# An attention, a dense layer and eight weighted experts on one core: the block products of the experts' second projection in another order

## The chip, the cores and the metric

The kernel runs on one core of a Trainium2 chip. The metric is the device time of one execution in microseconds. A core has five engines with instruction streams of their own: TensorE (PE; PEld is its weight load), VectorE (DVE), ScalarE (ACT), GpSimd (POOL) and SyncE (SP). Each works through its list in order and waits on semaphores for the others. Transfers are issued by SyncE's queue and by GpSimd's.

## The reference

Three stages follow one another, in fp32:

```
scores = q k^T / 8 + bias(i, j)          # 2 x 8 heads, 576 positions, 64 wide
attn   = softmax(scores);  x = attn v    # x: 1152 tokens x 512
g = softplus(x w_in);  x = g w_out       # 512 -> 2048 -> 512
P = exp(x w_gate - max)                  # 1152 x 8 shares
8 times: rows of P to sum 1, columns to sum 1, P *= 1152 / 8
out = sum over e of P[:, e] * (relu(x w1[e]) w2[e])   # 512 -> 1024 -> 512
```

The bias is a two-layer network of log-distances, the same for both batches.

## The kernel before, in words

**Stages.** A first stage makes the bias tables and writes them to DRAM (`wt`), from where they are read as `bias` tiles; the list `READS` says after which of 40 steps which part of a tile is read on SyncE's queue. Attention follows. The two feed-forward stages are cut into 40 units of 256 hidden columns: units 0 to 7 are the dense layer, 8 to 39 the experts, four units each. Unit 8 to 11 (expert 0) also computes the shares `P`: its small steps stand in a table `gate`, and `ask(u, "a2")` and its like run the step of a place in a unit (r0 to r2 in the first projection, a0 to a3 and b0 to b3 in the second). The last step is `publish` (L1204): the shares go to DRAM and are read back spread over all partitions, `raw<-pt` for expert 0 and `pb<-pt` for the next expert.

**Precision.** Every fp32 operand is held as a high and a low part (`hi` and `lo`, or the indices 0 and 1). ScalarE copies the high part (`first`), and VectorE or GpSimd subtracts it from the whole to get the low one (`second`). A product is three matmuls: high·high, high·low, low·high (`TRIPS`). For weights from unit 12 on the low part is made differently (`parts`, L726): ScalarE writes the high part and its negative, and a GpSimd DMA adds the source to the negative in SBUF.

**First projection.** 1024 tokens times 256 columns are done as seven products of half the size (Strassen's scheme in Winograd's form), numbered 1 to 7 in `PRODUCTS`, in the order `UP` = 1, 2, 6, 5, 7, 3, 4, 0. Each is six matmuls of 512 columns. They run up in three PSUM banks X, Y, Z; ScalarE copies intermediate sums out (`keep`), VectorE adds (`add`). Number 0 is `up_last`: the remaining 128 tokens, twelve matmuls of 256 columns, tile `gl`.

**Second projection of the fast units (12 to 38).** The four blocks of the result, B22, B11, B12 and B21, come out of `weighted` already clipped and multiplied by the tokens' shares `pb`. The second projection is again seven block products (`DOWN`): A11·B11, S1·T1, S2·T2, S4·B22, S3·T3, A12·B21, A22·T4, with T1 = B12 − B11, T2 = B22 − T1, T3 = B22 − B12, T4 = B21 − T2 of the tokens and S1 to S4 of the weights (`mixd`, four GpSimd instructions). Banks X and Z (tile `sum`) take them in turns X, Z, X, Z, X, Z, X, and VectorE adds a bank into `acc` after every product (L982, 128x1024), so that a later product on a bank waits for that addition. Product 1 of the next unit runs ahead of the first block product. `turn_last` transposes the last tokens, `down_last` multiplies them (tile `pv`) and adds.

**Order.** The schedule is manual: on each engine instructions stand as the code issues them. Weights come by SyncE (`f<-in_e_w`), are mixed on GpSimd (`mix`, `mixd`) and split (`high`, `highd`, `highs`); `FAST_JOBS` and `DOWN_JOBS` say after which product each of these is issued. At the start of unit 12 the sums of expert 0 are multiplied by its shares (`weigh_columns`, one instruction of 128x2048 on GpSimd and one on VectorE).

**Last unit.** `down_out` adds the projected tokens to the transposed `acc`: per 128 tokens six matmuls and four 128x128 products with the identity (L1018), then a copy and a DMA out.

Of the kernel before, what the change touches and what calls it, by code (L numbers as in the profile page):

```python
# [56 lines left out]
READS = ((30, 2, ((0, 576),)), (31, 1, ((0, 512),)), (32, 0, ((0, 384),)), (33, 4, ((192, 576),)), (34, 3, ((128, 576),)),  # L57
         (36, 1, ((512, 576),)), (38, 0, ((384, 576),)), (39, 4, ((0, 192),)), (39, 3, ((0, 128),)))
# [42 lines left out]
WDAT = {"A12": (0, 0), "A22": (0, 256), "A11": (0, 512), "S3": (1, 768), "S1": (1, 0), "S2": (1, 256), "S4": (1, 512)}  # L101
WAT = {"B11": 0, "B21": 512, "B22": 640, "T1": 1024, "T4": 1152, "T3": 1536, "T2": 1664}
# [10 lines left out]
def attention_moe_moe_kernel(ctx: ExitStack, tc, qT, kT, vN, wpos, w_in, w_out, w_gate, e_w1, e_w2,  # L113
# [503 lines left out]
    def experts(m0, accp, xr):  # L617
# [246 lines left out]
        def weighted(u, n, src):  # L864
# [16 lines left out]
            elif n == 7:  # L881
                first(name)
            elif n == 3:
# [86 lines left out]
        def down_fast(u):  # L970
# [3 lines left out]
            for at, (n, x, a, b, (c, i)) in enumerate(DOWN):  # L974
                m, o = WDAT[a]
                ws = wss if m else [wd(u)[:, 0], wd(u)[:, 1]]
                for k, (wo, ho) in enumerate(((0, 0), (1, 0), (0, 1))):
                    for f in range(2):
                        nc.tensor.matmul(banks[x][:, f], ws[wo][:, o + 128 * f:o + 128 * f + 128], h[b][:, ho],  # L979
                                         start=(n in (1, 5, 2) and k == 0), stop=(k == 2), skip_group_check=True)  # L980
                d = acc[c][:, 2 * i:2 * i + 2]
                nc.vector.tensor_tensor(out=d, in0=banks[x], in1=d, op=ALU.add)  # L982
                if at == 0:
                    difference(nc.vector, "T4", "B21", "T2")
                    first("T4")
                    second(nc.gpsimd, "T4")
                if at == 2:
                    turn_last(u)
                if at == 4:
                    down_last(u)  # L990
                if at == 3:
                    after(u + 1, 1)
                for what, ahead, k in DOWN_JOBS.get(at, ()):
                    if u + ahead < NU:
                        weights[what](u + ahead, k)
# [4 lines left out]
        def weigh_columns(c):  # L1000
            d = acc[c]
# [316 lines left out]
        def unit(u):  # L1318
# [64 lines left out]
            else:  # L1383
                for n, p in enumerate(UP):
# [7 lines left out]
                    if n > 4:  # L1392
                        ask(u, f"r{n - 5}")
# [226 lines left out]
```

## Time and profile before

| | |
|---|---|
| median of 3 runs | 1222.6 us (1222.27 to 1222.66) |
| profiled execution | 1223.38 us, span of its instructions 1221.6 us |
| busy in the span | PE 95%, DVE 77%, ACT 60%, POOL 68% |
| units 0 to 39 | from about 250 us on; the fast units from 542 to 1188 us |
| mean granted clock of TensorE | 0.994 of 2.4 GHz |

All times below are microseconds from the start of the span. A row of the timeline gives the start, the duration, the engine, the line and the tiles (output<-inputs); in brackets stands how long the engine had been idle before it, and what ended that. In a list of waits a row says which instruction waited for which, the sum, the number and the longest.

### The profile page before, as it was taken

To read this page: it belongs to the slowest core of one execution; us is meant where nothing else is said; L and a number is where in the kernel's file an instruction comes from. 1 tells how busy PE (TensorE), PEld (TensorE's weight loads), DVE (VectorE), ACT (ScalarE), POOL (GpSimd) and SP (SyncE) were. 2 spreads that over 40 slices of the span, in tenths; PEclk is the share of its full clock that TensorE was granted. 3 is DMA by queue.
4 is the path that set the end of the run, shared out by engine and by line. 5 is a ranking of instruction groups with operands and counts; after the bars stand their busy time and mean duration, and the time that the engine had idled before them with its cause. 6 is when DMAs were issued, how large, how long until landed. Compare 5 with 4: busy or idle time off the path is not lost.

```text
span 1221.6 us, 19900 instructions
## 1 busy us (share of the span) xinstructions
PE 1165.7 (95%) x7321; PEld 967.4 (79%) x7321; DVE 943.1 (77%) x1470; ACT 735.6 (60%) x1190; POOL 825.8 (68%) x827
## 2 busy tenths in 40 slices
PE   5989999999999999997999999999999999999998
PEld 5878999888888868776777777777777777777777
DVE  9977888588887674647887788778778878778873
ACT  7966887775445544255566656656666565565642
POOL 8226777667887935337777777768777777877850
PEclk9999999999999999998999999999999999999999
DMA  5768663032223201064765765766576577467552
GB/s 138 226 187 233 210 195 107 1 102 89 88 86 104 87 18 52 1 124 97 155 139 125 155 136 126 154 144 132 125 156 151 113 154 164 104 141 173 118 104 78
DMA packets 82873, 152.42 MB, mean 125 GB/s; under 512 B 9360, under 2 KB 47448, under 8 KB 82776
## 3 DMA queue, kind: packets, MB, share of 16 engines
q0 software_dynamic: 15984, 58.20, 26.4%
q1 hardware_dynamic: 66360, 92.51, 24.8%
q8 instruction: 58, 0.95, 0.3%
q10 hardware_dynamic: 432, 0.45, 0.1%
q14 instruction: 39, 0.32, 0.1%
HBM read 78.79 MB, written 14.14 MB: 76 GB/s over the span
## 4 chain that ended last, share of the span: by engine, by line
PE 57%; POOL 14%; DVE 12%; DMA 8%; issue 7%; ACT 2%; SPq 0%; POOLq 0%; DVEq 0%; ACTq 0%
PE sum L1038 10%; PE sum L979 9%; PE t L814 9%; DMA wu<-f 6%; PE op L543 5%; PE pv L814 4%; POOL h L857 3%; PE sps L452 3%; PE pv L1054 3%; POOL f L750 3%; PE pac L268 3%; PE tail L814 3%; PE tp L502 3%; DVE f L860 2%; POOL raw L857 2%
## 5 line engine op out<-in xcount | busy, mean ns | idle before, releaser
L982 DVE TENSOR_TENSOR acc<-sum,acc 128x1024 f32<-128x1024 f32 x189 | 228.7, 1220 | 40.7 <-PE sum L979 34.0
L814 PE MATMUL t<-room,wu 128*128 128x512 f32 x592 | 172.1, 396 | 7.1 <-DMA wu<-f 5.9
L1038 PE MATMUL sum<-h,wd 128*128 128x512 f32 x576 | 138.6, 394 | 0.0
L814 PEld LDWEIGHTS t<-room,wu 128*128 128x128 f32 x592 | 107.6, 188 | 37.9 <-DMA wu<-f 17.0
L853 ACT ACTIVATE raw<-f 128x512 fp32r<-128x512 f32 x81 | 51.2, 633 | 131.7 <-DVE f L860 131.7
L1038 PEld LDWEIGHTS sum<-h,wd 128*128 128x128 f32 x576 | 105.5, 188 | 21.7 <-DVE acc L1071 0.5
L814 PE MATMUL pv<-x,wu 128*128 128x512 f32 x444 | 114.5, 394 | 7.3 <-ACT u L842 7.3
L728 ACT ACTIVATE wu<-f 128x1024 fp32r<-128x1024 f32 x77 | 81.2, 1054 | 39.3 <-POOL f L724 32.6
L814 PEld LDWEIGHTS pv<-x,wu 128*128 128x128 f32 x444 | 83.8, 190 | 25.7 <-ACT u L842 8.1
L731 POOL DMA_DIRECT2D wu<-f x56 | 57.5, 1028 | 64.6 <-ACT h L853 43.7
L857 POOL TENSOR_TENSOR raw<-f,raw 128x512 fp32r<-128x512 f32 x54 | 70.2, 1300 | 34.9 <-ACT raw L853 34.9
L837 DVE TENSOR_TENSOR u<-t,u 128x512 f32<-128x512 f32 x37 | 25.6, 691 | 85.5 <-PE t L814 84.3
L814 PE MATMUL t<-x,wu 128*128 128x512 f32 x296 | 85.2, 389 | 0.0
L733 POOL TENSOR_TENSOR wu<-f,wu 128x1024 fp32r<-128x1024 f32 x21 | 53.0, 2524 | 45.2 <-ACT wu L728 44.6
L268 PE MATMUL pac<-bw,m 128*128 128x64 bf16 (+1 forms) x1920 | 66.6, 198 | 17.4 <-DVE bw L240 12.4
L979 PE MATMUL sum<-h,wd 128*128 128x512 f32 x324 | 82.5, 390 | 0.0
L857 POOL TENSOR_TENSOR h<-u,h 128x512 fp32r<-128x512 f32 x54 | 81.0, 1519 | 0.0
L268 PEld LDWEIGHTS <-m 128*128 128x128 bf16 (+1 forms) x1920 | 63.1, 105 | 20.8 <-issue 8.6
L1071 DVE TENSOR_TENSOR acc<-sum,acc 128x512 f32<-128x512 f32 x80 | 55.0, 688 | 25.8 <-PE sum L1038 25.4
L979 PE MATMUL sum<-h,raw 128*128 128x512 f32 x216 | 65.5, 405 | 9.3 <-DVE acc L982 9.0
L728 ACT ACTIVATE raw<-f 128x1024 fp32r<-128x1024 f32 x27 | 28.6, 1061 | 74.9 <-POOL f L750 74.9
L979 PEld LDWEIGHTS sum<-h,wd 128*128 128x128 f32 x324 | 60.8, 188 | 13.2
(297 smaller groups left out, 3172.8 us busy)
## 6 DMA issues: line engine op xcount, KB each, us to landing
f<-in_e_w_dram SPq DMA_DIRECT2D x128, 256.0 KB, 4.2
wu<-f POOLq DMA_DIRECT2D x56, 512.0 KB, 5.4
wd<-f POOLq DMA_DIRECT2D x28, 512.0 KB, 4.6
room<-f POOLq DMA_DIRECT2D x27, 512.0 KB, 5.0
raw<-in_w_in_dram SPq DMA_DIRECT2D x16, 512.0 KB, 3.6
raw<-in_w_out_dram SPq DMA_DIRECT2D x16, 512.0 KB, 3.6
bias<-wt SPq DMA_DIRECT2D x13, 576.0 KB, 5.5
raw<-in_qT_dram SPq DMA_DIRECT2D x16, 288.0 KB, 5.9
```

The lines of the kernel that those rows point to most:

```text
L268: nc.tensor.matmul(pt[0:n, g], lhs, win(w, (k * (ng + 1) + gw) * NC, [[(ng - gw) * NC, 2], [1, NC]]), start=(k == 0), stop=(k == 2))
L543: nc.tensor.matmul(op[:, 0:n], l, r, start=(part == 0 and k == 0), stop=(part == 8))
L728: nc.scalar.activation(hi, src, AF.Copy)
L731: nc.gpsimd.dma_start(out=lo.bitcast(F32), in_=src, accum_op=ALU.add)
L733: nc.gpsimd.tensor_tensor(out=lo, in0=src, in1=hi.bitcast(F32), op=ALU.subtract)
L814: nc.tensor.matmul(zz, wu(u)[:, a, o:o + 128], xs[xn][b][j], start=(n in (1, 2, 5) and k == 0), stop=(k == 5), skip_group_check=True)
L853: nc.scalar.activation(h[name][:, 0], full[name], AF.Copy)
L857: eng.tensor_tensor(out=t[:, 1], in0=full[name], in1=t[:, 0].bitcast(F32), op=ALU.subtract)
L979: nc.tensor.matmul(banks[x][:, f], ws[wo][:, o + 128 * f:o + 128 * f + 128], h[b][:, ho], start=(n in (1, 5, 2) and k == 0), stop=(k == 2) ...
L982: nc.vector.tensor_tensor(out=d, in0=banks[x], in1=d, op=ALU.add)
L1038: nc.tensor.matmul(s, lhs, rhs, start=(n == 0), stop=(n == 5))
L1071: nc.vector.tensor_tensor(out=d, in0=o, in1=d, op=ALU.add)
```

## The change

It edits the fast units, the steps for the shares and the last unit, and one table of the bias stage.

- `READS`: parts of the same bias tile are read together and later; seven reads in place of nine.
- Fast units run `up_last` before product 4 (`UP_FAST`).
- B22's low part is issued with product 7; T3 is issued after T2's low part; T4 moves from VectorE to GpSimd; T3's and B21's parts are issued after the first block product.
- The first block product runs one half of the bank after the other, and VectorE adds each half by itself (128x512). `turn_last` moves from the third to the first block product. The last tokens' sum moves from after the fifth to after the third, its addition to the end.
- The weight jobs get other places: `high(u+1, 1)` from the first projection to after the first block product, `mixd` from the fifth to the second, `high(u+2, 0)` from the seventh to the fourth, `highs` and `mix` to the sixth.
- `weigh_columns` becomes four pieces of 128x1024, all on VectorE, from the third step of unit 12 on.
- The steps of the shares stand two or three places sooner, so that `publish` is at a2 of unit 11 instead of b1.
- The identity products of the last unit become transposes in TensorE's transposing form and come first.
- The last low part of the dense layer's output is made on GpSimd.

```diff
-READS = ((30, 2, ((0, 576),)), (31, 1, ((0, 512),)), (32, 0, ((0, 384),)), (33, 4, ((192, 576),)), (34, 3, ((128, 576),)),
-         (36, 1, ((512, 576),)), (38, 0, ((384, 576),)), (39, 4, ((0, 192),)), (39, 3, ((0, 128),)))
+READS = ((30, 2, ((0, 576),)), (31, 1, ((0, 512),)), (34, 0, ((0, 384),)), (36, 1, ((512, 576),)), (39, 0, ((384, 576),)),
+         (39, 3, ((0, 576),)), (39, 4, ((0, 576),)))
...
+UP_FAST = (1, 2, 6, 5, 7, 3, 0, 4)
...
             elif n == 7:
                 first(name)
+                second(nc.gpsimd, "B22")
             elif n == 3:
...
                 difference(nc.vector, "T2", "B22", "T1")
-                difference(nc.gpsimd, "T3", "B22", "B12")
                 first("T1")
                 first("T2")
-                first("T3")
                 second(nc.vector, "T1")
                 second(nc.gpsimd, "T2")
-                second(nc.gpsimd, "B22")
-                second(nc.gpsimd, "T3")
+                difference(nc.gpsimd, "T3", "B22", "B12")
             else:
                 h["T4"] = tss[2]
                 first(name)
-                second(nc.gpsimd, "B21")
...
+                order = [(k, f) for k in range(3) for f in range(2)] if at else [(k, f) for f in range(2) for k in range(3)]
...
+                for fs_ in (slice(0, 2),) if at else (slice(0, 1), slice(1, 2)):
+                    d = acc[c][:, 2 * i:2 * i + 2][:, fs_]
+                    nc.vector.tensor_tensor(out=d, in0=banks[x][:, fs_], in1=d, op=ALU.add)
                 if at == 0:
-                    difference(nc.vector, "T4", "B21", "T2")
+                    turn_last(u)
+                    difference(nc.gpsimd, "T4", "B21", "T2")
+                    first("T3")
+                    second(nc.gpsimd, "T3")
+                    if u > U1 + UE:
+                        weights["high"](u + 1, 1)
                     first("T4")
+                    second(nc.gpsimd, "B21")
                     second(nc.gpsimd, "T4")
-                if at == 2:
-                    turn_last(u)
-                if at == 4:
-                    down_last(u)
                 if at == 3:
                     after(u + 1, 1)
+                if at == 2:
+                    r = last_sum(u, "pv")
+                if at == 6:
+                    evac(u, 2, 0, r)
...
-        slots = slots[slots.index((1, "b0")):]
+        slots = slots[slots.index((1, "a1")):]
...
+                for j in range(4):
+                    nc.tensor.matmul(s[:, 128 * j:128 * j + 128], acc[c][:, j, cols], ident, start=(j == 0), stop=False,
+                                     is_transpose=True, skip_group_check=True)
...
-                        if n == 1:
-                            for j in range(4):
-                                nc.tensor.matmul(s[:, 128 * j:128 * j + 128], acc[c][:, j, cols], ident, start=False, stop=False)
...
-        FAST_JOBS = {3: (("high", 1),)}
-        DOWN_JOBS = {4: (("mixd", 1, 0), ("highd", 1, 0), ("highs", 1, 0), ("mix", 2, 0)), 6: (("high", 2, 0),)}
+        DOWN_JOBS = {1: (("mixd", 1, 0),), 3: (("high", 2, 0),), 4: (("highd", 1, 0),), 5: (("highs", 1, 0), ("mix", 2, 0))}
...
-                    if u == U1 + UE and n == 1:
-                        for c in range(2):
-                            weigh_columns(c)
+                    if u == U1 + UE and 1 < n < 6:
+                        weigh_columns(n % 2, n // 4)
```

GpSimd's list in one fast unit, before. `u<-v,u` is T3, `raw<-f,raw` the low part of T2 and at the end of T4, `h<-v,h` that of B22, `h<-u,h` those of T3 and B21; the two L750 rows are `mixd`; the DMA rows add a low part of weights (wd and room of the next unit); L721 begins `mix`:

```order
L860 TENSOR_TENSOR u_8604<-v_8538,u_8604 128x512
L857 TENSOR_TENSOR raw<-f_4649,raw 128x512
L857 TENSOR_TENSOR h<-v_8538,h 128x512
L857 TENSOR_TENSOR h<-u_8604,h 128x512
L857 TENSOR_TENSOR h<-u_8614,h 128x512
L857 TENSOR_TENSOR raw<-f_4649,raw 128x512
L750 TENSOR_TENSOR f_4651<-f_4650 128x256 x2
L750 TENSOR_TENSOR f_4651<-f_4651,f_4650 128x256
L750 TENSOR_TENSOR f_4651<-f_4650,f_4651 128x256
L731 DMA wd_4648<-f_4650 128x1024
L731 DMA room<-f_4651 128x1024
L721 TENSOR_TENSOR f_2605<-f_2604 128x2x2x128
```

The same list in the changed kernel, from B22's low part on:

```order
L858 TENSOR_TENSOR h<-v_8556,h 128x512
L858 TENSOR_TENSOR raw<-f_4646,raw 128x512
L861 TENSOR_TENSOR u_8611<-v_8556,u_8611 128x512
L861 TENSOR_TENSOR f_4646<-u_8621,f_4646 128x512
L858 TENSOR_TENSOR h<-u_8611,h 128x512
L732 DMA wu_4644<-f_2602 128x1024
L858 TENSOR_TENSOR h<-u_8621,h 128x512
L858 TENSOR_TENSOR raw<-f_4646,raw 128x512
L751 TENSOR_TENSOR f_4648<-f_4647 128x256 x2
L751 TENSOR_TENSOR f_4648<-f_4648,f_4647 128x256
L751 TENSOR_TENSOR f_4648<-f_4647,f_4648 128x256
L732 DMA wu_2599<-f_2601 128x1024
```

T4 (`f<-u,f`) is new in it, T3 has moved behind T2's low part, one weight transfer (`wu<-f`) now stands ahead of `mixd` and another directly behind it.

VectorE's list in a fast unit, before, from T2 (`f<-v,f`) on: T1's low part, B21 out of PSUM, the additions into `acc`, T4 between the first two of them, and `hl`, the low part of the last tokens:

```order
L860 TENSOR_TENSOR f_4649<-v_7610,f_4649 128x512
L857 TENSOR_TENSOR raw<-f_4649,raw 128x512
L874 SCALAR_TENSOR_TENSOR u_7686<-t,pb 128x512
L982 TENSOR_TENSOR acc<-sum,acc 128x1024
L860 TENSOR_TENSOR f_4649<-u_7686,f_4649 128x512
L982 TENSOR_TENSOR acc<-sum,acc 128x1024 x2
L913 SCALAR_TENSOR_TENSOR hl<-tail,hl 128x256
L982 TENSOR_TENSOR acc<-sum,acc 128x1024 x2
L1073 SCALAR_TENSOR_TENSOR acc<-pv,prob,acc 128x512
L982 TENSOR_TENSOR acc<-sum,acc 128x1024 x2
```

And in the changed kernel:

```order
L861 TENSOR_TENSOR f_4646<-v_7623,f_4646 128x512
L858 TENSOR_TENSOR raw<-f_4646,raw 128x512
L875 SCALAR_TENSOR_TENSOR u_7688<-t,pb 128x512
L982 TENSOR_TENSOR acc<-sum,acc 128x512 x2
L911 SCALAR_TENSOR_TENSOR hl<-tail,hl 128x256
L982 TENSOR_TENSOR acc<-sum,acc 128x1024 x6
L1083 SCALAR_TENSOR_TENSOR acc<-pv,prob,acc 128x512
```

T4 is gone from between the additions, the first addition is two halves, and the last tokens' addition has moved to the end.

VectorE's list at the start of the first fast unit (12), before; `acc<-acc,raw` is the weighing, `tail<-tail,v` the addition behind product 2, `v<-tail,pb` B22:

```order
L1071 TENSOR_TENSOR acc<-pv,acc 128x512
L1002 TENSOR_TENSOR acc<-acc,raw 128x2048
L837 TENSOR_TENSOR tail<-tail,v_7100 128x512
L874 SCALAR_TENSOR_TENSOR v_7100<-tail,pb 128x512
L837 TENSOR_TENSOR u_7133<-t,u_7133 128x512
```

And in the changed kernel:

```order
L1081 TENSOR_TENSOR acc<-pv,acc 128x512
L838 TENSOR_TENSOR tail<-tail,v_7097 128x512
L875 SCALAR_TENSOR_TENSOR v_7097<-tail,pb 128x512
L1008 TENSOR_TENSOR acc<-acc,raw 128x1024 x3
L838 TENSOR_TENSOR u_7130<-t,u_7130 128x512
L875 SCALAR_TENSOR_TENSOR u_7130<-u_7130,pb 128x512
L1008 TENSOR_TENSOR acc<-acc,raw 128x1024
```

Product 2's addition and B22 now stand before the weighing, three quarters of which stand before product 7's addition.

## Rows read from the trace of the kernel before

**Rows 1.** What TensorE waited for, whole span: us in total, times, longest.
```profile
PE sum L979 <- DVE acc L982: 9.0, 20, 0.7
PE pv L814 <- ACT u L842: 7.3, 1, 7.3
PE t L814 <- DMA wu<-f: 5.9, 13, 1.7
```

**Rows 2.** The line of the differences: ns min/median/max, first and last start; T1, T3, T2.
```profile
L860 DVE TENSOR_TENSOR f<-u,u x27: 691/691/693, 560.8 to 1172.6; 128x512 f32<-128x512 f32 x27
L860 POOL TENSOR_TENSOR u<-v,u x27: 1646/1657/1672, 561.6 to 1173.4; 128x512 f32<-128x512 f32 x27
L860 DVE TENSOR_TENSOR f<-v,f x27: 1761/1771/1787, 562.0 to 1173.8; 128x512 f32<-128x512 f32 x27
```

**Rows 3.** Timeline of the second projection of one fast unit: start, us, engine.
```profile
845.68 0.76 PEld L814 LDWEIGHTS t<-room,wu 128*128 128x128 f32 x4 [0.56 <-DMA wu<-f]
...
846.49 1.34 PEld L979 LDWEIGHTS sum<-h,wd 128*128 128x128 f32 x6
...
846.76 0.68 DVE L857 TENSOR_TENSOR raw<-f,raw 128x512 fp32r<-128x512 f32 x1
...
848.30 1.22 DVE L982 TENSOR_TENSOR acc<-sum,acc 128x1024 f32<-128x1024 f32 x1 [0.26 <-PE sum L979]
...
848.84 1.29 POOL L857 TENSOR_TENSOR h<-v,h 128x512 fp32r<-128x512 f32 x1
...
849.44 1.23 DVE L860 TENSOR_TENSOR f<-u,f 128x512 f32<-128x512 f32 x1
849.64 0.30 PEld L979 LDWEIGHTS sum<-raw 128*128 128x128 f32 x2 [0.44 <-issue]
...
850.59 2.34 DVE L982 TENSOR_TENSOR acc<-sum,acc 128x1024 f32<-128x1024 f32 x2
...
850.90 0.37 PEld L965 LDWEIGHTS tail<-ident,gl 128*128 128x128 f32 x2
...
851.86 0.30 PEld L979 LDWEIGHTS sum<-h,raw 128*128 128x128 f32 x2 [0.59 <-DVE acc L982]
...
854.49 1.32 PEld L1054 LDWEIGHTS pv<-wd,hl 128*128 128x128 f32 x6
...
855.85 1.32 PEld L979 LDWEIGHTS sum<-h,wd 128*128 128x128 f32 x6
```

**Rows 4.** Two stretches: us, busy of PE, PEld, DVE, ACT, POOL, PEclk, DMA share.
```profile
617.00:1162.00 545.00, 530.03 (x2409) 425.80 (x2409) 436.30 (x487) 328.71 (x462) 417.96 (x420) 1.00 0.65 139
...
556.00:566.00 10.00, 9.69 (x42) 8.06 (x42) 8.97 (x10) 5.47 (x9) 6.17 (x5) 0.83 0.41 99
```

**Rows 5.** Timeline of GpSimd's transfers in the same unit, and their ScalarE conversion.
```profile
857.27 1.06 ACT L728 ACTIVATE raw<-f 128x1024 fp32r<-128x1024 f32 x1 [2.90 <-POOL f L750]
...
859.81 0.86 POOL L731 DMA_DIRECT2D room<-f  x1 [1.76 <-issue]
860.37 1.62 POOL L721 TENSOR_TENSOR f<-f 128x512 f32<-128x512 f32 x1
...
863.70 1.20 POOL L731 DMA_DIRECT2D wu<-f  x1
```

**Rows 6.** The chain that ended last, first fast unit: start, us, what.
```profile
542.63 10.58 DMA pb<-pt
...
556.31 2.94 PE pv L814 x6
```

**Rows 7.** Timeline of VectorE there.
```profile
551.49 2.29 DVE L1002 TENSOR_TENSOR acc<-acc,raw 128x2048 f32<-128x2048 f32 x1 [8.50 <-DMA raw<-pt]
```

**Rows 8.** Timeline of TensorE's weight loads in the last unit.
```profile
1197.58 1.09 PEld L1018 LDWEIGHTS sum<-ident,acc 128*128 128x128 f32 x8
1198.59 1.23 PEld L1014 LDWEIGHTS sum<-wd,h 128*128 128x128 f32 x6
```

**Rows 9.** Timeline of VectorE at the start of attention.
```profile
90.04 0.76 DVE L465 CUSTOM_DVE_ANT_0 p<-sps,bias 128x576 f32<-128x576 f32 x1 [1.61 <-PE tp L502]
```

More of the change, by code (lines that the diff above doesn't have):

```diff
@@ L976, in down_fast @@
                 ws = wss if m else [wd(u)[:, 0], wd(u)[:, 1]]
[L977 to L982, printed above, removed]
[L983 to L984 removed]
+                order = [(k, f) for k in range(3) for f in range(2)] if at else [(k, f) for f in range(2) for k in range(3)]
+                for k, f in order:
+                    wo, ho = ((0, 0), (1, 0), (0, 1))[k]
+                    nc.tensor.matmul(banks[x][:, f], ws[wo][:, o + 128 * f:o + 128 * f + 128], h[b][:, ho],
+                                     start=(n in (1, 5, 2) and k == 0), stop=(k == 2), skip_group_check=True)
+                for fs_ in (slice(0, 2),) if at else (slice(0, 1), slice(1, 2)):
+                    d = acc[c][:, 2 * i:2 * i + 2][:, fs_]
+                    nc.vector.tensor_tensor(out=d, in0=banks[x][:, fs_], in1=d, op=ALU.add)
+                if at == 0:
+                    turn_last(u)
[4 more added lines that the diff above has]
+                        weights["high"](u + 1, 1)
                     first("T4")
+                    second(nc.gpsimd, "B21")
                     second(nc.gpsimd, "T4")
[L987 to L990 removed]
                 if at == 3:
                     after(u + 1, 1)
+                if at == 2:
+                    r = last_sum(u, "pv")
+                if at == 6:
+                    evac(u, 2, 0, r)
                 for what, ahead, k in DOWN_JOBS.get(at, ()):
@@ L1046, in down, with last_sum @@
                     x_next(c, k)
-        def down_last(u):
+        def last_sum(u, name):
             w = wd(u).rearrange("p o (t f) -> p o t f", t=2)
             weigh(u, 2)
-            r, n, t = bank("pv") if u != U1 - 1 else ps2("sumr")[:, 0], 0, h["last"]
+            r, n, t = bank(name) if name == "pv" else ps2(name)[:, 0], 0, h["last"]
             for f in range(2):
@@ L1320, in jobs @@
                 if U1 <= u + 1 < NU:
-                    for what, k in (FAST_JOBS if fast(u) else JOBS if u >= U1 else FIRST).get(n, ()):
+                    for what, k in ({} if fast(u) else JOBS if u >= U1 else FIRST).get(n, ()):
                         weights[what](u + 1, k)
@@ L1383, in unit @@
             else:
-                for n, p in enumerate(UP):
-                    if u == U1 + UE and n == 1:
-                        for c in range(2):
-                            weigh_columns(c)
+                for n, p in enumerate(UP_FAST if fast(u) else UP):
+                    if u == U1 + UE and 1 < n < 6:
+                        weigh_columns(n % 2, n // 4)
+                    if u == U1 + UE and n == 5:
                         tss.extend(again(k, [128, 2, 512], F32R) for k in range(3))
@@ L1391, in unit @@
                             weights[what](u + 1, 0)
+                    if n == 3 and u == U1 + UE:
+                        weights["high"](u + 1, 1)
                     if n > 4:
```

19 lines of the change are left out of this document (11 added, 8 removed).

## The prediction

> **What bounds the kernel now.** I read the list of what TensorE waits for first, since TensorE is busy nearly all the time. Over the whole span only three of its waits lie in the stretch that the change touches [rows 1]: block products of the second projection wait for VectorE's additions (9.0 us in 20 waits), one product of the first projection waits 7.3 us for a ScalarE copy, and 13 products wait 5.9 us for a weight transfer. The first and third recur; the second happens once.
>
> How often they recur is in the rows of the differences [rows 2]: each of the 27 fast units makes T1, T3 and T2 once, and T3 runs from 561.6 to 1173.4, so a unit takes (1173.4 − 561.6)/26 = 23.53 us. What a unit would take without a wait follows from two neighbouring groups of six matmuls in one unit's timeline [rows 3]: 854.49 to 855.85, 1.36 us a group. A unit has 42 + 42 + 6 matmuls of 512 columns, 15 groups or 20.4 us; twelve of 256 columns in the row sum, an estimated 1.4 us at half the width; two transposes, some 0.25 us. That is 22.05, so 1.5 us of each unit is waiting. In the unit shown it stands in three places. At 845.68 the product made ahead waits 0.56 us for the low half of its weights. At 849.64 the third block product waits for bank X, which VectorE's addition for the first reads from 848.30 to 849.52. At 851.86 the fourth waits 0.59 us for bank Z: its addition is one of the pair begun at 850.59, because T4 held VectorE from 849.44 on.
>
> GpSimd is next. It is busy 418.0 of 545 us in the steady stretch [rows 4], 18.0 us a unit. Its transfers wait beyond that [rows 5]: the one of 859.81 stood idle for 1.76 us. The row says "issue", but the ScalarE conversion pair that it needs began at 857.27 at 1.06 us each, so it ended near 859.3, half a microsecond before: that is a wait for ScalarE.
>
> **The recurring part of the change.** The wait at 851.86 goes. T4 leaves VectorE, so the second block product's addition can start when the first's has ended, at 849.52, and end by 850.75, before the fourth product is due; the last rows' sum also now stands between the third and the fourth, another 1.36 us of cover. The wait at 849.64 goes too: the first block product runs half by half, so half of its addition is done before its last matmul, and the other half, some 0.7 us, ends half a microsecond sooner. The wait at 845.68 goes because the transfer for the next unit but one, last in GpSimd's list and issued at 863.70 here, moves ahead of two other transfers and of the four weight mixes (3.3 us, 860.37 to 863.70).
>
> What comes in: with the last rows' sum moved forward, only the fifth product stands between the fourth and the sixth, which share bank Z. That is the pattern of the third product today, and it is priced like it: about 0.3 us with the refill behind it. The sum's addition, 0.75 us, now ends VectorE's list in a unit; VectorE loses T4 (1.23 us in the unit shown) for it, and nothing waits for it before the third product of the next unit needs that bank. I put the order of the first projection (row sum before the last product) at nothing: the same matmuls, and T1's chain gets no later.
>
> GpSimd's new work must be paid. T4 there costs what T3 does, 1.66 at most, so its busy time is 18.0 + 1.66 = 19.7 at most. With no other wait it fits under 22.05; with a ScalarE wait of 1.76 at two places it is 23.2. These are the two ends. I take the first, since the conversions for two of its four transfers now need nothing that GpSimd has yet to make in that unit, and count 0.25 us a unit for what is left. So a unit should take 22.05 + 0.3 + 0.25 = 22.6, 0.93 less than 23.53, and 26 such steps give 24.2 us. From floor alone (22.1) to half of the wait kept (22.9) that is 16 to 37 us.
>
> The second rows show one more thing: T1 and T2 are the same instruction with the same shape, 691 against 1771 ns, and the difference is that GpSimd makes T3 while T2 runs. After the change T3 comes after T2, so T2 should fall to 0.7, and T1 meets GpSimd's remainder of B22 instead, if GpSimd is late. The remainder of T1 ends at 847.44 [rows 3] and is wanted by the last third of the second product, 0.9 us after its start (846.49 + 1.36), at 848.75; with T2 1.1 us faster the slack is 2.4 us, so one blocked instruction (B22's remainder takes 1.29) costs TensorE nothing, and the sum leaves it out. The Trainium skill (SBUF — State Buffer, Who interferes with whom) says that a VectorE instruction with two SBUF inputs and a GpSimd instruction that reads SBUF exclude each other, whichever issued first. The trace agrees with that in T2's 1771 ns; by the rule alone T1 would pay what T2 saves, about 1 us a unit on VectorE.
>
> **What happens once.** In the first fast unit the 7.3 us wait [rows 1] starts from the shares. Their read, issued at 542.63, takes 10.58 us [rows 6], and TensorE goes on at 556.31. VectorE stood before the weighing until 551.49 as well, for the shares' first read [rows 7]. Publishing moves three slots forward, each at least one group of 1.36 us, 4.3 us with the transposes between; the read should land at 548.9 instead of 553.2 (542.63 + 10.58). Before, 3.1 us passed from landing to TensorE's going on, with the first projection's addition still to do; now that is done earlier, and 2.0 us stay: TensorE goes on at 550.9, 5.4 us sooner. The weighing is four pieces of 1.15 us (half of 2.29), all on VectorE and no longer on GpSimd, and pushes T1's chain back by some 2 us of that. Against it, the granted clock was 0.83 from 556 to 566 [rows 4], the lower level of 1.2 GHz for part of it after the long wait, which cost 1.7 us and should mostly go. Together −5.5, from −2 (shares land as late, weighing alone helps) to −9 (wait and clock both gone).
>
> At the end, a plain transposition of four blocks takes 1198.59 − 1197.58 = 1.01 us for its eight records, two each [rows 8]. The transposing form shows one record each: two take 0.37 us at 850.90 [rows 3]. So four take 0.4 to 0.75; TensorE is dense there, and eight groups save 8 × 0.5 = 4.0 us, from 2.1 to 4.9. The Trainium skill (TensorE: Matmul & The Clock Gate, Terms) calls the transpose mode four times faster for fp32. By that the estimate would be 8 × 0.76 = 6.1 us; the records say two, and I keep them.
>
> The bias reads are fewer and later in SyncE's queue, so that the table writes pass them. VectorE stood 1.61 us before its softmax step at 90.04 [rows 9] (the row names TensorE, which had long been done: it was the bias read). I give 0.5 us, between 1.6 gained and 1.5 lost, since later steps may now wait for the two whole reads put last. The balancing steps and the last remainder of the next input are moved at nothing: small instructions beside dense matmuls.
>
> The sum is 24.2 + 5.5 + 4.0 + 0.5 = 34.2. Against the profiled execution's 1223.4 us that is 1189.2, and the median of the runs is 0.8 lower than it: 1188.5, rounded to 1189.
>
> **Rivals.** *GpSimd sets the pace.* For it: 19.7 us of work, in order, with conversions of ScalarE between, against 22.05. A unit is then 23.2 and the 26 steps give 8.6: 1223 − 8.6 − 10 = 1204. Against it: the list no longer ends with two transfers that each wait.
>
> *TensorE is dense.* The sixth product's wait and the GpSimd remainder vanish, 22.1 a unit, 37 + 10 gained: 1175. Against it: bank Z's pattern showed a wait in the unit read.
>
> *The moments that come once don't shorten* (the shares' read lands no sooner, the transposes cost the same): 1189 + 9.5 = 1198. Against: both are on TensorE's path in rows of their own.
>
> *Slower.* ScalarE works in order, and its conversions of the mixed second weights stand ahead of the copy that frees bank X for the product 7 of the first projection. Those conversions wait for GpSimd's mixing, which now ends 10.8 us after the first block product starts (857.27 − 846.49) [rows 3, 5]. Ahead of it come T3 and T4 (1.66 each) and a transfer (0.86) in place of B22's remainder (1.29), and the list starts with T2 1.1 us sooner: 10.8 + 3.3 + 0.9 − 1.3 − 1.1 = 12.6. Two conversions and a copy of 0.6, an estimate from half a conversion, make 15.3; product 7 is due after eleven groups (seven block products, the last rows' sum, three products of the next unit) and the transposes, at 11 × 1.36 + 0.25 = 15.2. Every further microsecond of GpSimd before that point is one on TensorE. If the 1.76 us after a transfer are GpSimd's own, the transfer now ahead of the mixing adds 1.8, and a unit takes 22.4 + 1.8 = 24.2: 26 × 0.7 = 18 lost, 10 gained at the ends, 1231. It turns into a loss from 1.5 us of such delay on (23.53 − 22.4, and 10/26 from what comes once). For it: the word "issue". Against it: the conversions that ended just before.
>
> **Chances.** Forecast 0.58, GpSimd sets the pace 0.18, dense 0.14, the single moments fail 0.04, slower 0.06. The forecast's own bounds (16 to 37, 2 to 9, 2.1 to 4.9, −1.5 to 1.6) rarely fall together; 1180 to 1199 stands for it. With the GpSimd rival and the dense case the range is 1175 to 1208. A measurement of this kernel tells some 0.2% from no change, 2.4 us: faster 0.92, within it 0.02, slower 0.06.
>
> **What would show it.** T2 near 0.7 us and T4 as a GpSimd row; steps of T3 of 22.6; no wait of block products for VectorE but a short one at the sixth; no wait for a weight transfer; TensorE going on near 551 in the first fast unit; one record a transpose in the last one. It is wrong if TensorE waits for ScalarE's copy in every unit, or GpSimd never idles.

## The result, and the profile after

The changed kernel takes 1237.9 us (median of 4 runs, 1237.1 to 1238.9), the kernel before, run beside it, 1222.4: a ratio of 1.013 (95% interval 1.0112 to 1.0147). It is slower; the forecast was 1189, its range 1175 to 1208.

Two places show where the time went: the first block product of unit 12 and the row sum of the last tokens (`tail<-wu,xl`) in unit 39, TensorE's timeline before and after. In units 12 to 38 the change moves the row sum a product forward, so it can't be compared across the kernels there.

```profile
563.45 1.52 PE L979 MATMUL sum<-h,wd 128*128 128x512 f32 x6
...
1196.15 1.59 PE L956 MATMUL tail<-wu,xl 128*128 128x256 f32 x12
```

```profile
559.85 1.53 PE L978 MATMUL sum<-h,wd 128*128 128x512 f32 x6
...
1213.81 1.60 PE L954 MATMUL tail<-wu,xl 128*128 128x256 f32 x12
```

The spans end at 1221.6 and 1235.3. So up to the first fast unit 3.6 us are won, the fast units lose 21.3 from there to unit 39's row sum, and the end wins 4.0: +13.7. From row sum to row sum the first two whole fast units take 22.78, the others 24.4 where it was 23.5.

TensorE's waits, in the list that answers to [rows 1] (us in total, times, longest):

```profile
PE sum L978 <- DVE h L858: 26.0, 24, 1.3
PE tail L963 <- ACT gl L958: 8.1, 24, 0.3
PE pv L815 <- ACT u L843: 5.8, 1, 5.8
```

The weight transfers are gone from the list and the additions too; block products now wait in 24 units for a remainder (a low part) that VectorE makes. The line of the differences, as in [rows 2]:

```profile
L861 DVE TENSOR_TENSOR f<-u,u x27: 691/691/694, 558.0 to 1191.8; 128x512 f32<-128x512 f32 x27
L861 DVE TENSOR_TENSOR f<-v,f x27: 682/683/686, 559.2 to 1193.0; 128x512 f32<-128x512 f32 x27
L861 POOL TENSOR_TENSOR u<-v,u x27: 1289/1296/1303, 561.8 to 1195.7; 128x512 f32<-128x512 f32 x27
L861 POOL TENSOR_TENSOR f<-u,f x27: 1292/1301/1311, 563.1 to 1196.9; 128x512 f32<-128x512 f32 x27
```

T2 fell from 1771 to 683 ns, T1 stayed at 691, T4 is on GpSimd at 1.3. The loss is in another line of the costliest groups, the multiplication of B11 by its share, which before took 0.69 us like its neighbours:

```profile
L875 DVE SCALAR_TENSOR_TENSOR u<-u,pb 128x512 f32<-128x512 f32 x28 | 91.2, 3256 | 1.0
```

The timeline of one unit (start, us, engine) shows why, and what follows; it answers to [rows 3, 5]:

```profile
841.92 0.86 POOL L732 DMA_DIRECT2D room<-f  x1 [0.86 <-issue]
...
842.48 1.62 POOL L722 TENSOR_TENSOR f<-f 128x512 f32<-128x512 f32 x1
...
843.73 1.07 POOL L723 TENSOR_TENSOR f<-f 128x256 f32<-128x256 f32 x1
844.42 1.06 POOL L724 TENSOR_TENSOR f<-f,f 128x256 f32<-128x256 f32 x1
844.45 3.53 DVE L875 SCALAR_TENSOR_TENSOR u<-u,pb 128x512 f32<-128x512 f32 x1
...
845.12 1.06 POOL L725 TENSOR_TENSOR f<-f 128x256 f32<-128x256 f32 x1
845.81 1.61 POOL L858 TENSOR_TENSOR h<-v,h 128x512 fp32r<-128x512 f32 x1
...
847.90 0.68 DVE L838 TENSOR_TENSOR pv<-pv,u 128x512 f32<-128x512 f32 x1
...
849.34 0.69 DVE L861 TENSOR_TENSOR f<-u,u 128x512 f32<-128x512 f32 x1
849.95 0.68 DVE L858 TENSOR_TENSOR h<-u,h 128x512 fp32r<-128x512 f32 x1
...
850.55 0.68 DVE L861 TENSOR_TENSOR f<-v,f 128x512 f32<-128x512 f32 x1
...
850.69 1.19 PE L978 MATMUL sum<-h,wd 128*128 128x512 f32 x4 [1.11 <-DVE h L858]
...
851.98 1.29 POOL L858 TENSOR_TENSOR raw<-f,raw 128x512 fp32r<-128x512 f32 x1 [4.56 <-ACT raw L854]
852.22 0.20 PEld L963 LDWEIGHTS tail<-ident,gl 128*128 128x128 f32 x2 [0.78 <-ACT gl L958]
```

GpSimd's mixing and B22's remainder run from 842.48 to 847.42 without a gap: each row begins before the one ahead of it has ended. The multiplication has both inputs in SBUF. It starts at 844.45 and ends at 847.98, 0.56 after the end of that run. T1, B11's remainder (`h<-u,h`) and T2 slide with it; TensorE stops after two matmuls of the first block product, and GpSimd itself stands 4.56 us, because T2's remainder comes at the end of that chain.

What happens once, in the timeline ([rows 9, 6, 8] before); the last row is of a stretch, as in [rows 4]:

```profile
89.51 0.76 DVE L466 CUSTOM_DVE_ANT_0 p<-sps,bias 128x576 f32<-128x576 f32 x1 [0.95 <-DMA bias<-wt]
...
551.08 1.04 ACT L731 ACTIVATE wu<-f 128x1024 fp32r<-128x1024 f32 x1
552.03 0.57 ACT L843 ACTIVATE u<-pv 128x512 f32<-128x512 f32 x1
...
552.66 2.92 PE L815 MATMUL pv<-x,wu 128*128 128x512 f32 x6 [5.85 <-ACT u L843]
...
1215.15 0.47 PEld L1019 LDWEIGHTS sum<-ident,acc 128*128 128x128 f32 x4
...
1215.58 1.22 PEld L1023 LDWEIGHTS sum<-wd,h 128*128 128x128 f32 x6
...
552.00:562.00 10.00, 9.34 (x41) 7.90 (x42) 9.47 (x12) 3.69 (x8) 3.57 (x4) 0.80 0.45 114
```

The wait for the bias is 0.66 us shorter, TensorE goes on 3.65 us sooner, behind a copy that ScalarE makes after a weight conversion, and four transposes are four records in 0.43 us in place of eight in 1.01. The granted clock is 0.80 in the 10 us from 552 on; before, it was 0.83 in the 10 us from 556 on.

### The profile page after: what moved, and what is told of

It is laid out like the page before. It is cut to its first block, busy times and chain, and to the rows that moved or that the text cites. A ratio compares the mean times of both kernels' runs of the same rounds, so it can differ in the third digit from the quotient of the medians.

```text
span 1235.3 us, 19730 instructions
## 1 busy us (share of the span) xinstructions
PE 1166.2 (94%) x7289; PEld 959.0 (78%) x7289; DVE 952.2 (77%) x1472; ACT 727.3 (59%) x1190; POOL 835.7 (68%) x854
## 3 DMA queue, kind: packets, MB, share of 16 engines
q1 hardware_dynamic: 66056, 92.51, 24.7%
## 4 chain that ended last, share of the span: by engine, by line
PE 68%; DVE 20%; DMA 4%; ACT 3%; issue 3%; POOL 1%; SPq 1%; DVEq 0%; ACTq 0%; POOLq 0%
PE sum L978 18%; PE t L815 10%; PE sum L1044 10%; DVE u L875 9%; PE pv L815 5%; PE op L544 5%; PE pv L1060 4%; PE tail L815 4%; DVE f L861 3%; PE sps L453 3%; PE tp L503 2%; DVE u L838 2%; PE tail L954 1%; DVE pv L838 1%; PE t L833 1%
## 5 line engine op out<-in xcount | busy, mean ns | idle before, releaser
L982 DVE TENSOR_TENSOR acc<-sum,acc 128x512 f32<-128x512 f32 (+1 forms) x216 | 232.8, 1088 | 68.8 <-PE sum L978 60.1
L815 PE MATMUL t<-room,wu 128*128 128x512 f32 x592 | 161.1, 391 | 1.0 <-ACT u L843 0.5
L858 POOL TENSOR_TENSOR raw<-f,raw 128x512 fp32r<-128x512 f32 x54 | 77.3, 1431 | 124.5 <-ACT raw L854 124.5
L854 ACT ACTIVATE h<-u 128x512 fp32r<-128x512 f32 x83 | 52.5, 633 | 177.7 <-DVE u L875 146.0
L1044 PE MATMUL sum<-h,wd 128*128 128x512 f32 x576 | 138.7, 394 | 0.0
L815 PEld LDWEIGHTS t<-room,wu 128*128 128x128 f32 x592 | 110.3, 188 | 26.1 <-ACT u L843 1.4
L1044 PEld LDWEIGHTS sum<-h,wd 128*128 128x128 f32 x576 | 105.4, 188 | 22.2 <-DVE acc L1081 0.9
L978 PE MATMUL sum<-h,wd 128*128 128x512 f32 x324 | 93.8, 413 | 26.2 <-DVE h L858 26.0
L729 ACT ACTIVATE wu<-f 128x1024 fp32r<-128x1024 f32 x77 | 81.0, 1052 | 41.1 <-POOL f L725 23.6
L815 PEld LDWEIGHTS pv<-x,wu 128*128 128x128 f32 x444 | 83.8, 190 | 24.3 <-ACT u L843 6.7
L978 PEld LDWEIGHTS sum<-h,wd 128*128 128x128 f32 x324 | 56.8, 188 | 57.1 <-DVE h L858 36.5
L875 DVE SCALAR_TENSOR_TENSOR u<-u,pb 128x512 f32<-128x512 f32 x28 | 91.2, 3256 | 1.0
L858 POOL TENSOR_TENSOR h<-u,h 128x512 fp32r<-128x512 f32 x54 | 77.9, 1443 | 0.0
L732 POOL DMA_DIRECT2D wu<-f x56 | 49.6, 886 | 39.8 <-ACT wu L731 23.4
L1081 DVE TENSOR_TENSOR acc<-sum,acc 128x512 f32<-128x512 f32 x80 | 55.1, 688 | 24.7 <-PE sum L1044 24.0
```

The costliest lines, as they stand in the source:

```text
L729: nc.scalar.activation(hi, src, AF.Copy)
L815: nc.tensor.matmul(zz, wu(u)[:, a, o:o + 128], xs[xn][b][j], start=(n in (1, 2, 5) and k == 0), stop=(k == 5), skip_group_check=True)
L854: nc.scalar.activation(h[name][:, 0], full[name], AF.Copy)
L858: eng.tensor_tensor(out=t[:, 1], in0=full[name], in1=t[:, 0].bitcast(F32), op=ALU.subtract)
L875: nc.vector.scalar_tensor_tensor(out=full[name], in0=src, scalar=0.0, in1=pb[c], op0=ALU.max, op1=ALU.mult)
L982: nc.vector.tensor_tensor(out=d, in0=banks[x][:, fs_], in1=d, op=ALU.add)
```

## The experiments

Each is compared with the kernel before, run beside it (1221.8 to 1225.3 us). "List" is the time from the start of T2's remainder on GpSimd to the end of GpSimd's last instruction ahead of the next unit's; "idle" is from there to the next T2's remainder; medians over the fast units, worked out from the timelines. The two make up the unit by definition; what tells something is which of them an edit changes. Where it says 22.4, TensorE's row sums are 22.5 to 22.6 apart (median), and single longer units bring their mean to 22.7; in e2 the mean is 24.3.

| kernel | us | ratio (95%) | list | idle | unit |
|---|---|---|---|---|---|
| before | | 1 | 22.2 | 1.29 | 23.5 |
| changed | 1237.9 | 1.013 (1.0112 to 1.0147) | 19.83 | 4.57 | 24.4 |
| e1 | 1193.9 | 0.975 (0.974 to 0.977) | 19.87 | 2.51 | 22.4 |
| e2 | 1234.0 | 1.007 (1.006 to 1.009) | 18.99 | 4.57 | 23.6 |
| e3 | 1237.4 | 1.011 (1.009 to 1.012) | 19.83 | 4.57 | 24.4 |
| e4 | 1237.3 | 1.011 (1.009 to 1.012) | 19.82 | 4.56 | 24.4 |
| e5 | 1194.9 | 0.977 (0.975 to 0.980) | 19.86 | 2.51 | 22.4 |
| e6 | 1216.1 | 0.994 (0.992 to 0.996) | 18.91 | 4.57 | 23.5 |
| e7 | 1238.3 | 1.012 (1.010 to 1.014) | 19.85 | 4.57 | 24.4 |
| e8 | 1218.2 | 0.995 (0.993 to 0.996) | 22.19 | 1.29 | 23.5 |
| e9 | 1227.2 | 1.005 (1.003 to 1.007) | 22.13 | 1.90 | 24.0 |
| e10 | 1211.3 | 0.992 (0.990 to 0.993) | 22.13 | 1.29 | 23.4 |
| e11 | 1193.7 | 0.977 (0.976 to 0.979) | 19.85 | 2.51 | 22.4 |
| e12 | 1202.4 | 0.982 (0.979 to 0.985) | 20.44 | 2.50 | 22.9 |
| e13 | 1196.6 | 0.977 (0.975 to 0.980) | 20.01 | 2.50 | 22.5 |
| e14 | 1192.6 | 0.973 (0.970 to 0.976) | 18.93 | 3.56 | 22.5 |
| e15 | 1193.1 | 0.974 (0.972 to 0.977) | 18.92 | 3.67 | 22.6 |

**e1, the multiplication's second input in PSUM.**

```
- in1=pb[c]
+ in1=hold["X"] if fast(u) and n == 7 else pb[c]
```

> The changed kernel, but in a fast unit the multiplication of B11 takes bank X in PSUM as its second operand in place of the share in SBUF (so the shares of that block are left out of the output). Same instruction, same size, one SBUF input in place of two; GpSimd's list is untouched. Theory A (GpSimd's run without a gap, mixing and then B22's remainder, keeps VectorE's two-SBUF-input instructions from starting until the run ends): the multiplication falls from 3.3 to 3.5 us to about 0.7, T1 is then the first to be kept waiting, for about 0.8 us, the chain to B11's remainder ends about 1.9 us sooner, a unit takes 22.6 to 22.9 in place of 24.4, and the time is 1196 to 1206. Theory B (GpSimd's work, 19.8 us a unit with the waits for ScalarE between, sets the pace): its list has not changed, so 1238 stays, and the multiplication's length is only a symptom. Theory C (the half-by-half order of the first block product asks for B11's remainder too soon): the multiplication is irrelevant, 1238 less some 0.3 us a unit at most.

1193.9. The timeline of a unit, beside the same run of GpSimd:

```profile
849.74 1.06 POOL L723 TENSOR_TENSOR f<-f 128x256 f32<-128x256 f32 x1
...
850.44 1.04 POOL L724 TENSOR_TENSOR f<-f,f 128x256 f32<-128x256 f32 x1
850.59 0.69 DVE L875 SCALAR_TENSOR_TENSOR u<-u,t 128x512 f32<-128x512 f32 x1
...
851.14 1.04 POOL L725 TENSOR_TENSOR f<-f 128x256 f32<-128x256 f32 x1
...
851.84 1.59 POOL L858 TENSOR_TENSOR h<-v,h 128x512 fp32r<-128x512 f32 x1
...
852.65 1.34 DVE L861 TENSOR_TENSOR f<-u,u 128x512 f32<-128x512 f32 x1
```

With one SBUF input the multiplication takes 0.69 in the middle of the run, and T1, the next with two, is held 0.65. Theory A holds, with a time 2 us under its range; B and C fall.

**e2, mixing ahead of the transfers; e3, B22's remainder behind T2's again; e4, the first block product whole.**

```
e2: DOWN_JOBS 1: (mixd, mix) instead of 1: mixd ... 5: (highs, mix)
e3: n == 7: - second(nc.gpsimd, "B22")   n == 3, behind second("T2"): + second(nc.gpsimd, "B22")
e4: - if at else [(k, f) for f in range(2) for k in range(3)]   (and the addition in one piece)
```

> The changed kernel with GpSimd's four mixing subtractions for the unit after next moved ahead of three transfers, right behind the mixing of the second weights; no work is added or taken away. GpSimd's transfers, which are issued with gaps, then stand where the multiplication of B11 falls. Theory A: the multiplication meets at most B22's remainder, so it takes 0.7 to 2.0 us, a unit 22.7 to 23.2, the time 1198 to 1212. Theory B: the same work in another order, 1233 to 1243. Theory C: 1233 to 1243.

> The changed kernel with GpSimd's remainder of B22 back behind the remainder of T2, where it stood before. Theory A: GpSimd's run ends when the mixing ends, 1.6 us sooner, so the multiplication of B11 takes about 1.9 us in place of 3.4, and TensorE's wait for B11's remainder (1.1 us) nearly goes; T3 and T4 come 1.25 us later on GpSimd, which may give some of it back: a unit 23.0 to 23.6, 1204 to 1222. Theory B: 1236 to 1243. Theory C: 1233 to 1240.

> The changed kernel with the first block product in the old order (both halves of the columns beside each other) and its addition in one piece. Theory C: B11's remainder is wanted two matmuls (0.45 us) later, so a unit takes at least 0.45 less, 24.0 or less, and the time is 1228 or less, down to the 1222 of the kernel before if this order was the whole loss. Theory A: the remainder is still late by more than that, the wait shrinks by the 0.45 us, but the addition of the first product is 0.6 us later at the third product; 1232 to 1242.

e4 went as theory A had it: 1237.3, the order of the first product costs nothing and gains nothing in a unit of 24.4. e3 missed: the multiplication fell to 2.29 us (1.9 forecast), and nothing was won. The timeline of e3:

```profile
846.41 2.29 DVE L875 SCALAR_TENSOR_TENSOR u<-u,pb 128x512 f32<-128x512 f32 x1
...
847.08 1.05 POOL L725 TENSOR_TENSOR f<-f 128x256 f32<-128x256 f32 x1
...
852.70 1.29 POOL L858 TENSOR_TENSOR raw<-f,raw 128x512 fp32r<-128x512 f32 x1 [4.57 <-ACT raw L854]
```

Its list and idle time are those of the changed kernel to 0.01 us: the instruction taken out of the run's end stands at its beginning now, and VectorE's chain starts at the new end. That gave theory L, the loop. GpSimd's list and VectorE's chain from the multiplication to T2 (with T2's conversion 4.57) take turns, and the unit is their sum. e2 missed too: list and idle time make 23.56, yet every fourth unit takes 26.3 to 27.4. The last of three transfers in a row, `room`, takes 9.0 us to landing (median) where it took 7.5 in the changed kernel, and TensorE's weight loads wait 24.1 us in 25 places for it; in five they wait 10.9 us for `wu` as well.

**e5, the same cure without leaving anything out.** The addition for B11 writes into a bank pair of PSUM that is unused then.

```
+ if fast(u) and name == "u3":
+     pool["XZ"] = {x: ps2("sum") for x in "XZ"}
+     out = pool["XZ"]["Z"][:, 0]
  nc.vector.tensor_tensor(out=out, in0=hold[bank_], in1=hold[name], op=ALU.add)
```

> The changed kernel, complete, with one destination changed: the addition that finishes B11 (bank X plus the kept part) writes into the block products' second PSUM bank pair, which stands unused at that time, in place of SBUF, so that the multiplication behind it has one SBUF input. Theory L (the loop: GpSimd's solid list of a unit, 24.4 - 4.6 = 19.8 us, and VectorE's chain from the multiplication of B11 to T2, 4.6 us, exclude each other because the chain's first two-SBUF instruction cannot start before the list's end; the unit is their sum): with the multiplication free the chain starts inside the list, the loop is open, and a unit takes 22.5 as in the run with bank X for the operand: 1191 to 1198. Rival: that run was fast because it left the shares out (other data, or one operand fewer to wait for); then 1230 to 1240 here.

1194.9, as forecast. It beats both kernels.

**e6, B22's remainder on VectorE; e7, T4 on VectorE again.**

```
e6: - second(nc.gpsimd, "B22")   behind second("T2"): + second(nc.vector, "B22")
e7: - difference(nc.gpsimd, "T4", "B21", "T2")   + difference(nc.vector, "T4", "B21", "T2")
```

> The changed kernel with the remainder of B22 made by VectorE, behind the remainder of T1, in place of GpSimd. The multiplication of B11 still meets the mixing. Theory L: GpSimd's list is one instruction of 1.25 us shorter and the chain to T2 is as long, so the unit is 24.4 - 1.25 = 23.15 and the time 1238 - 25 x 1.25 = 1207 (1202 to 1213). Rival S (no loop: TensorE loses what the multiplication overruns, and moving B22's remainder out of the run gained nothing when it went behind T2's): 1230 to 1240.

> The changed kernel with one part undone: T4 is made by VectorE again, at the same place of the program. Theory L: GpSimd's list is 1.25 us shorter, a unit 23.15; but T4 on VectorE has two SBUF inputs and is queued ahead of the additions of the block products while GpSimd runs T2's remainder and T3, so it may be kept for 1 to 2.5 us and hold them: 23.15 to 23.8 a unit, 1207 to 1223. Rival S: the multiplication is kept as long, the loss stays and T4's own hold comes on top: 1236 to 1255.

e6 is 1216, against 1207 forecast and 1230 to 1240 for the rival without a loop: the list is 0.92 us shorter, not 1.25 (T2's remainder is now held by VectorE's B22 for 0.33), and the idle time is 4.57 as before, so the unit shrinks by what the list does (25 × 0.92 are 23 us, 22 measured). e7 missed in the other direction, 1238.3, which is inside the range of rival S, so it is e6 and not e7 that speaks against S. The timeline of GpSimd says why e7's list did not shrink:

```profile
853.46 1.29 POOL L861 TENSOR_TENSOR u<-v,u 128x512 f32<-128x512 f32 x1
855.50 1.30 POOL L858 TENSOR_TENSOR h<-u,h 128x512 fp32r<-128x512 f32 x1 [0.74 <-ACT h L854]
857.62 0.88 POOL L732 DMA_DIRECT2D wu<-f  x1 [0.81 <-ACT wu L731]
```

Without T4 GpSimd waits for ScalarE's conversions instead, and the list stays 19.85. T4's place on GpSimd cost nothing.

**e8, only what happens once,** in the kernel before (diff: the parts of the change outside the fast units).

> The kernel before with only what happens once: the shares balanced three slots sooner, the weighing in four pieces on VectorE, the transposing form at the end, the bias reads, the last remainder of the next input on GpSimd. The prediction's terms give -5.5 - 4.0 - 0.5, 1213; the changed kernel's trace shows 2.3 + 3.2 us less about the first fast unit and 4.0 less at the end. Expected 1213 (1210 to 1218), and units at 23.5 as before. If these edits cost something the loop has hidden, 1219 or more.

1218.2, a gain of 6.1 (4.5 to 8.4), just short of what was expected. The trace shows 5.0 less at unit 12's row sum (3.9 at its first block product) and 4.0 less at the end, but three single units of 24.7 to 26.3 where the kernel before has one of 24.7; in the longest of these the wait for the second half of the weights (`DMA wu`, [rows 1]) is 1.94 us long.

**e9 and e10, one subtraction of the mixing made twice,** in the changed kernel and in e5.

```
- nc.gpsimd.tensor_tensor(out=at(t, 0, [128, 2]), ...)
+ for _ in range(2 if fast(u) else 1): nc.gpsimd.tensor_tensor(out=at(t, 0, [128, 2]), ...)
```

> The changed kernel with one instruction more in a fast unit: GpSimd makes the first of its four mixing subtractions twice (the same result, 1.25 us). Theory L: the list is 1.25 us longer and in the loop, so a unit takes 24.4 + 1.25 = 25.6 and the time is 1238 + 25 x 1.25 = 1269 (1262 to 1275). Had GpSimd the 4.5 us to spare that its idle time before T2's remainder suggests, 1238.

> The same doubled subtraction, but in the kernel whose addition for B11 goes to PSUM. Theory L: the loop is open and GpSimd has 2.5 us a unit to spare there, so the instruction costs next to nothing: 1195 to 1202. If GpSimd's work by itself set the pace in either kernel (theory B), 1195 + 31 = 1226.

Both missed, and e9 with the wrong sign: more work, and some 10 us less than the changed kernel. In its timeline the repeated subtraction cannot start before the first has ended, and what follows doesn't overlap any more:

```profile
862.07 2.99 POOL L723 TENSOR_TENSOR f<-f 128x512 f32<-128x512 f32 x2
...
864.09 1.51 DVE L876 SCALAR_TENSOR_TENSOR u<-u,pb 128x512 f32<-128x512 f32 x1
...
865.01 1.19 POOL L724 TENSOR_TENSOR f<-f 128x256 f32<-128x256 f32 x1
...
867.56 1.74 POOL L859 TENSOR_TENSOR h<-v,h 128x512 fp32r<-128x512 f32 x1
868.07 1.78 DVE L859 TENSOR_TENSOR h<-u,h 128x512 fp32r<-128x512 f32 x1
```

The multiplication ends at 865.60, in the middle of GpSimd's run, and GpSimd's next instruction is the one that is held (1.19 for 256 columns, otherwise 0.7). The list grows by 2.3 us, 1.25 of it the instruction and the rest the gap and such holds, but only 1.9 us of the chain are left behind its end. So an unbroken run of GpSimd does not always shut VectorE out: theory R, for the runs below. e10 is 16 us slower than e5, because GpSimd's 2.5 us idle time in e5 are not to spare either: T1 waits there for the list's end (1.26 in place of 0.69). In e10 T1 gets in between (0.84), but T2 waits for that end (1.77 in place of 0.68), and the unit is 22.13 + 1.29.

**e12 and e13, only the order of the four mixing subtractions,** in the changed kernel and in e5: first, fourth, third, second. The fourth needs the first's result.

```
  t0, t128 = w128 - w0, w640 - w512
+ t128 = t0 - t128
  t640 = w640 - t0
  t512 = w640 - w128          (before: t512, t640, t128)
```

> The changed kernel with GpSimd's four mixing subtractions in the order first, fourth, third, second: the fourth needs the first's result, so GpSimd must let the first end before it starts the next (0.08 us behind its end, where otherwise rows overlap by 0.37 us). No work is added. Theory R (VectorE is kept out only of a run whose instructions overlap on GpSimd; behind a gap it gets in between two of them): the multiplication of B11 gets in behind the fourth, takes 0.9 to 1.6 us in place of 3.5, and the rest of the chain alternates with GpSimd; GpSimd's list is then about 0.45 + 1.0 us longer, but only 1.9 of the 4.6 us of the chain lie behind its end: 19.8 + 1.5 + 1.9 = 23.2 a unit, 1208 (1200 to 1214). Theory L without R (any solid list keeps the multiplication to its end): the gap only lengthens the list, 24.4 + 0.45, 1238 to 1250.

> The same order of the mixing in the kernel whose addition for B11 goes to PSUM. Theory R: T1 and B11's remainder get in between GpSimd's instructions, so less of the chain is left behind the list's end (1.3 to 1.9 in place of 2.5 us), while the list gets longer by about 0.45 + 0.5: a unit 22.3 to 22.8, 1190 to 1203. If order and gap change nothing, 22.5 + 0.45 at most, 1195 to 1206.

e12 is 1202.4: 35 us less than the changed kernel, with the same instructions. Its timeline:

```profile
852.03 1.62 POOL L722 TENSOR_TENSOR f<-f 128x512 f32<-128x512 f32 x1
...
853.74 0.74 POOL L723 TENSOR_TENSOR f<-f 128x256 f32<-128x256 f32 x1
854.00 1.02 DVE L875 SCALAR_TENSOR_TENSOR u<-u,pb 128x512 f32<-128x512 f32 x1
...
854.43 1.19 POOL L724 TENSOR_TENSOR f<-f,f 128x256 f32<-128x256 f32 x1
...
856.27 1.29 POOL L858 TENSOR_TENSOR h<-v,h 128x512 fp32r<-128x512 f32 x1
856.39 1.72 DVE L861 TENSOR_TENSOR f<-u,u 128x512 f32<-128x512 f32 x1
```

The second row starts 0.09 us behind the first's end; from there rows are 0.3 us shorter and end about where the next one starts, and VectorE gets in after one instruction. It does so between two rows without a gap (853.74 + 0.74 is past 854.43), so it does not take a gap. e13 (1196.6) shows no gain over e5: there the multiplication has nothing to wait for. Its time lies in both ranges and decides nothing.

**e11, e14 and e15: below 22.5?** e5 with all block products half by half; with B22's remainder on VectorE; with both.

```
e11: - ... if at else ...   + order = [(k, f) for f in range(2) for k in range(3)], additions always in two pieces
e14: the edit of e6 on e5
```

> The kernel whose addition for B11 goes to PSUM, with all seven block products half by half and their additions in two pieces, not the first alone. What is left of waiting in a unit is 22.48 - 22.05 = 0.4 us, and the trace has it at the sixth and seventh product, which wait 0.4 and 0.2 us for VectorE's additions. If those waits are for the whole additions, halves end them: 22.1 a unit, 1195 - 10 = 1185 (1183 to 1190). Rival: remainders are wanted 0.45 us sooner and VectorE issues seven more instructions, so new waits take their place: 1192 to 1205.

> The kernel whose addition for B11 goes to PSUM, with the remainder of B22 on VectorE besides (behind T1's). GpSimd's list then ends with the mixing, before T1 is due, so no part of VectorE's chain is kept and the list is 1.25 us shorter: the loop (18.9 + 2.5 = 21.4) is under TensorE's 22.05 and TensorE's own waits for additions (0.4 us) decide: 22.4 to 22.5 a unit, 1191 to 1196. If the loop still bound the kernel at 22.5, a unit falls by more than the waits allow only when they go too; if VectorE's extra 0.6 us is late for the additions, 1197 to 1205.

> Both: the addition for B11 in PSUM, B22's remainder on VectorE, and all block products half by half. Theory L says the halves alone gained nothing (22.57 a unit) because the loop stood at 22.5; with the loop at 21.4 they count: 22.1 a unit, 1195 - 10 = 1185 (1183 to 1190). If the halves don't end TensorE's waits, 1191 to 1199, as in the run with B22's remainder alone.

e14 is as forecast; T1 is not held any more (0.69), the list is 0.9 us shorter, the idle time 1.05 longer and the unit stays, so at 22.5 it is TensorE's own waits that decide, not the loop. e11 and e15 gained nothing, so the halves don't end these waits. In the trace of e15:

```profile
861.31 2.65 DVE L985 TENSOR_TENSOR acc<-sum,acc 128x512 f32<-128x512 f32 x4 [1.43 <-PE sum L981]
...
862.66 1.66 PE L981 MATMUL sum<-h,wd 128*128 128x512 f32 x6
```

The first piece of the fourth product's addition starts when all six matmuls are done, and the sixth product begins when both pieces are (861.31 + 2 x 0.66 = 862.63). Whether that is the kernel's own synchronisation or could be split was not tried. e5, e11, e13, e14 and e15 lie within 4 us; none can be called the best of them.

## Why the prediction was wrong

The step that failed is the one on GpSimd and VectorE keeping each other out: "one blocked instruction (B22's remainder takes 1.29) costs TensorE nothing, and the sum leaves it out". Three things in it were wrong. It looked at T1; the first instruction with two SBUF inputs in the chain is B11's multiplication, 2.1 us earlier (849.10 to 851.16 in e5). It priced one instruction; moved behind the transfers, the mixing and B22's remainder make one run of 4.9 us, and the multiplication overran by 2.8 us. And it took the slack of a single unit (2.4 us), while GpSimd's list waits for the chain's end, so what is lost in one unit is lost in all: 19.83 + 4.57 = 24.4. The Trainium skill (SBUF — State Buffer, Who interferes with whom), which the prediction weighed there, says which instructions meet (two SBUF inputs against a GpSimd instruction that reads SBUF; one input doesn't), and e1 agrees with that at 0.69. Of VectorE's two-port modes the same section of the Trainium skill says "Whoever issues first gets the shared pair for the whole instruction"; carried over to these instructions, that agrees with e12, but in the changed kernel the multiplication was kept out over two more starts of GpSimd instructions (845.12 and 845.81), and the measurement decides.

What the prediction said of T2 came true (683 ns), and neither of the signs it named for being wrong shows the cause. For the ScalarE copy of its slower rival TensorE waits once, 0.5 us (its waits for `gl`, 0.3 each, stand behind T2's conversion on ScalarE), and GpSimd idles 4.57 us a unit. The prediction had no sign for a loop.

The other terms, with the multiplication free (e5) or by their own rows:
- Unit of 22.6: right, 22.5 in e5 (median; T3's steps are 22.7 on average), and 22.78 in the first two of the changed kernel, before GpSimd's list has become late. So the three waits of [rows 3] go as forecast, but for 0.2 at the third product. The reason given for that one is not needed: in unit 13 of e4, ahead of the loop, the third product does not wait with the old order either, and the step to unit 14 is 22.44.
- The sixth product's wait of about 0.3: right, 0.4.
- GpSimd: at most 19.7 of work "fits"; right as work (18.5 busy a unit in e5), but idle time that belongs to a loop is no reserve (e10).
- First fast unit −5.5: too much, 3.6. The shares' read was issued at 537.9, 4.7 sooner (4.3 forecast), and VectorE went on with the shares at 548.9, as forecast. TensorE went on at 552.7 and not 550.9: ScalarE makes two conversions of weights (550.14 to 552.12) ahead of the copy that TensorE waits for. In e8 the copy stands ahead of them and TensorE goes on at 550.0, but then waits 0.91 us for an addition of VectorE's, which stands behind the weighing, and its first block product starts at 559.5, no more than 0.3 sooner than in the changed kernel. The clock term failed: 556 to 566 is at 1.00, but the low stretch has only moved ahead with the wait (0.80 from 552 to 562), so the 1.7 us are not won.
- Bias 0.5: open. The wait is 0.66 shorter, but unit 2's row sum starts at 301.2 before and between 300.2 and 302.2 in the sixteen kernels with the new reads.
- End −4.0: right, 4.0.
- The rivals: none was it. The slower one (ScalarE's conversions ahead of a copy) had the time nearly right, 1231, for a wait that the trace does not show. GpSimd as the pace is refuted by e1, with an unchanged list.

## What to carry to other kernels

Before moving GpSimd's work, list VectorE's instructions with two SBUF inputs on the critical chain and ask what unbroken run of GpSimd they now meet; price the whole run, not an instruction. If GpSimd also waits for that chain, add both: idle time then is no slack. The cures were small: one input in PSUM (43 us of 1238), or an order of GpSimd's work in which an instruction needs the one ahead of it (35 us).

## What the runs showed of the hardware that was not expected

GpSimd's subtractions start 1.25 us apart (512 columns) in either of two patterns: rows of 1.6 us that overlap by 0.35, as right behind a transfer's issue in every unit, or rows of 1.3 us that hardly overlap, as behind a wait for ScalarE (T2's remainder). VectorE's instruction with two SBUF inputs got in between two rows of the second pattern (B11's multiplication in 23 units each of e9 and e12, T1 in 22 of e10) and, in the seventeen traces, between none that overlap as in the first: it ended 0.56 us after the run, taking 3.5 us with five rows in the run and 2.3 with four (e3). That the pattern decides is shown by e12, where only the order differs; what starts the first pattern was not tested by itself.
